# Window attention and a top-1 mixture of experts: a PSUM fill moved to TensorE, routing arithmetic moved to GpSimd

## The chip, the cores and the metric

One core of one Trainium2 chip. The metric is the device time of one execution in microseconds; of several executions the median is given.

## The reference, cut to what matters

Eight batches, eight heads, 576 positions, head size 64. Attention looks back over a window of 64 positions; its result, 4,608 rows of 512 numbers, goes through a gate that picks one of eight experts for each row, and only that expert's two matrices are applied.

```python
scores = scale * (q @ k.T)                      # per batch and head
scores = where((rel >= 0) & (rel < 64), scores, -1e9)
attn = softmax(scores); x = (attn @ v) as [4608, 512]
logits = x @ w_gate                             # [4608, 8]
e = argmax(logits, 1); g = softmax(logits)[e]
out[rows of e] = g * (relu(x[rows of e] @ w1[e]) @ w2[e])
```

## The kernel before, in words

**Attention.** The positions are cut into chunks of 64; two chunks make a tile of 128 rows, and there are 36 tiles. Step i of a loop written out by hand (L825 and on) works on several tiles at once, and the order of its calls is the order of each engine's queue. `scores(i)` on TensorE writes, for each chunk, its products with the chunk in front of it (half 0) and with itself (half 1) into PSUM. `folded(i)` on VectorE copies half 1 over half 0 where the mask says so (L412), `largest(i)` takes the maximum. ScalarE makes the exponentials of tile i-1 (L428) and copies the transposed ones of tile i-2 to SBUF (`tsb`, L437); GpSimd multiplies these by two masks (`pm`, L444, two instructions in each step); TensorE makes the products with v for tile i-3 (`values`, L458), and VectorE divides and writes `xrow` (`shares`, L468), which goes to DRAM. TensorE then transposes rows of tile i-4 (L475) and makes gate logits for every fourth step (L519).

The first chunk of each batch has no chunk in front of it. For these eight chunks `folded` first fills half 0 of their 64 partitions with FILL = -8e9 by a VectorE memset (L411). They fall in tiles 0, 4, 9, 13, 18, 22, 27 and 31.

**Routing.** After tiles 16, 28 and 36 (rounds of 16, 12 and 8 tiles; called round 1, 2 and 3 here) `route` turns logits into the row's place within its expert. It is cut into pieces `s1` to `s8`, which the loop takes from a queue `slow`, two in a step during attention and up to four after it: s1 the maximum `lm`; s2 the difference `ld` and the candidates `eq`; s3 the choice, as one-hot `oh`; s4 running counts on TensorE; s5 and s6 positions `pos` and the sum of exponentials; s7 and s8 the place and the gate weight in three bf16 parts (`val`). Then a queue `puts`, one entry in a step during attention and two after it, holds `put` (one-hot rows of the place within a block, `hot_row`, L601, four tiles each) and `early_parts` (`said`, L617); `follow` sets the steps in which a table of the first experts' rows is made (`early_table`) and in which GpSimd gathers these rows (`xg`, L179).

**Experts.** The first four experts' first two blocks of rows are begun inside the loop from step 36 (`forward`), the rest follows. Each weight tile is split into a rounded part `whi` (ScalarE) and a remainder `wlo` (VectorE, L237), and each product is made of three (L307, L311, L278). A planning stage (`plan`, VectorE, small instructions) places the remaining blocks.

`SPACE` is a tile that is never used; it keeps later tiles at the addresses they have.

Of the kernel before, what the change touches and what calls it, by code (L numbers as in the profile page):

```python
# [24 lines left out]
P = 128  # L25
# [39 lines left out]
RATE = (2, 1)  # L65
PUT = 4
AHEAD = 2
SPACE = (232, 64)
SPLIT = 26
TURN = 36  # L70
LAST = 7
# [47 lines left out]
def window_attention_then_top1_moe(ctx: ExitStack, tc: tile.TileContext, qkv, wall, wg, cst, out):  # L119
# [35 lines left out]
    def cc(name):  # L155
        o, w = CO[name]
        return cs[0][:, o:o + w] if o < NFIRST else cs[1][:, o - NFIRST:o - NFIRST + w]
# [8 lines left out]
    ones = const.tile([P, P], BF16, name="ones")  # L166
    one8 = const.tile([P, E], F32, name="one8")
    ones_f = const.tile([P, P], F32, name="ones_f")
    base = const.tile([P, E], F32, name="base")
    const.tile([P, SPACE[0]], F32, name="space0")  # L170
    xg = [const.tile([P, WIDE, C], F32, name=f"xg{i}") for i in range(3)]
# [25 lines left out]
    class Weights:  # L197
# [11 lines left out]
        def load(self):  # L209
            jj = self.loaded  # L210
            if jj == NJ // 2:
                return
            self.loaded += 1
            raw = self.raws[jj] = wr.tile([P, 2, 2 * C], F32, name="raw")
            ev = self.ev
            src = wall[ev, jj] if isinstance(ev, int) else wall[bass.ds(ev, 1), jj].rearrange("o p j f -> p (o j) f")
            if jj < self.spread:
                at, gap = QUARTERS[jj]
                quarters.extend((at + gap * k, raw[:, k // 2, k % 2 * C:(k % 2 + 1) * C],
                                 src[:, k // 2, k % 2 * C:(k % 2 + 1) * C]) for k in range(4))  # L220
            else:
                nc.sync.dma_start(out=raw, in_=src)
# [140 lines left out]
    nc.sync.dma_start(out=cs[1], in_=cst[:, NFIRST:])  # L363
    for c in range(6, FIRST):
        load(c)
    nc.vector.tensor_copy(out=fold, in_=cc("fold"))
    nc.vector.memset(ones, 1.0)
    nc.vector.memset(one8, 1.0)
    nc.vector.memset(ones_f, 1.0)
    for t in xg:  # L370
        nc.gpsimd.memset(t, 0.0)

# [19 lines left out]
    def scores(n):  # L392
        sp = sp_of(n)
        for g in range(NG):
            for j in range(2):
                c = 2 * n + j
                r = c % RING
                for a in range(2):
                    rows, cols = slice(a * W, (a + 1) * W), slice(j * W, (j + 1) * W)
                    if c % NC:  # L400
                        nc.tensor.matmul(sp[cols, a, g], lhsT=q_r[rows, r, g], rhs=k_r[rows, r - 1:r + 1, g], start=True,  # L401
                                         stop=True)
                    else:
                        nc.tensor.matmul(sp[cols, a, g, 1], lhsT=q_r[rows, r, g], rhs=k_r[rows, r, g], start=True, stop=True)

    def folded(n):

        sp = sp_of(n).rearrange("p a g b w -> p (a g) b w")
        for j in range(2):
            if (2 * n + j) % NC == 0:  # L410
                nc.vector.memset(sp[j * W:(j + 1) * W, :, 0], FILL)  # L411
        nc.vector.copy_predicated(out=sp[:, :, 0], mask=fold.unsqueeze(1).to_broadcast([P, H, W]), data=sp[:, :, 1])  # L412

    def largest(n):
# [108 lines left out]
    def route(nt, lgs, t0, rnd):  # L523
        def b8(x):
            return x.unsqueeze(2).to_broadcast([P, nt, E])

        v = {}

        def new(name, w=None, dt=F32):
            v[name] = rt.tile([P, nt] + ([w] if w else []), dt, name=name)  # L530
            return v[name]

        def s1():
            nc.vector.tensor_reduce(out=new("lm"), in_=lgs, op=ALU.max, axis=AX.X)

        def s2():
            nc.vector.tensor_tensor(out=new("ld", E), in0=lgs, in1=b8(v["lm"]), op=ALU.subtract)

            nc.vector.scalar_tensor_tensor(out=new("eq", E), in0=v["ld"], scalar=0.0,
                                           in1=cc("desc").unsqueeze(1).to_broadcast([P, nt, E]),  # L540
                                           op0=ALU.is_ge, op1=ALU.mult)
            new("ex", E)
            exs.append(lambda: nc.scalar.activation(out=v["ex"], in_=v["ld"], func=AF.Exp))

        def s3():
            nc.vector.tensor_reduce(out=new("em"), in_=v["eq"], op=ALU.max, axis=AX.X)
            oh = v["oh"] = rt.tile([P, nt + 1, E], BF16, name="oh")
            nc.vector.memset(oh[:, nt], 0.0)
            nc.vector.tensor_tensor(out=oh[:, 0:nt], in0=v["eq"], in1=b8(v["em"]), op=ALU.is_equal)

        def s4():
            oh = v["oh"]
            rk = rest_b[:, 1, 0:(nt + 1) * E].rearrange("p (t e) -> p t e", e=E)
            nc.tensor.matmul(rk, lhsT=tri, rhs=oh, start=True, stop=False)
            for s in range(1, nt + 1):
                nc.tensor.matmul(rk[:, s:], lhsT=ones, rhs=oh[:, 0:nt + 1 - s], start=False, stop=(s == nt))
            rks = v["rks"] = rt.tile([P, nt + 1, E], F32, name="rks")
            nc.scalar.copy(out=rks, in_=rk)

        def s5():  # L560
            rks = v["rks"]
            nc.vector.tensor_tensor(out=new("pos", E), in0=rks[:, 0:nt],
                                    in1=base.unsqueeze(1).to_broadcast([P, nt, E]), op=ALU.add)
            nc.vector.tensor_tensor(out=base, in0=base, in1=rks[:, nt], op=ALU.add)
            if rnd in SNAP:

                k = SNAP[rnd] // 2 * E
                nc.vector.tensor_tensor(out=base, in0=base, in1=cc("elow")[:, k:k + E], op=ALU.max)

        def s6():  # L570
            nc.vector.tensor_reduce(out=new("se"), in_=v["ex"], op=ALU.add, axis=AX.X)
            nc.vector.tensor_tensor(out=v["pos"], in0=v["pos"], in1=v["oh"][:, 0:nt], op=ALU.mult)
            nc.gpsimd.tensor_scalar(out=v["se"], in0=v["se"], scalar1=1e-9, scalar2=None, op0=ALU.add)

        ts_ = slice(t0, t0 + nt)

        def s7():
            nc.vector.tensor_reduce(out=new("pf2"), in_=v["pos"], op=ALU.add, axis=AX.X)
            nc.vector.reciprocal(out=new("g"), in_=v["se"])
            nc.gpsimd.tensor_scalar(out=new("fl"), in0=v["pf2"], scalar1=1.0 / P, scalar2=129.0 / 256,  # L580
                                    op0=ALU.mult, op1=ALU.add)
            nc.gpsimd.tensor_scalar(out=mid[:, ts_], in0=v["fl"], scalar1=RND, scalar2=RND + 1, op0=ALU.add,
                                    op1=ALU.subtract)

        def s8():
            nc.vector.scalar_tensor_tensor(out=new("lo"), in0=mid[:, ts_], scalar=float(-P), in1=v["pf2"],
                                           op0=ALU.mult, op1=ALU.add)

            nc.gpsimd.tensor_copy(out=val[:, ts_, 2], in_=v["g"])
            nc.gpsimd.tensor_tensor(out=new("g1"), in0=v["g"], in1=val[:, ts_, 2], op=ALU.subtract)  # L590
            nc.gpsimd.tensor_copy(out=val[:, ts_, 3], in_=v["g1"])
            nc.gpsimd.tensor_tensor(out=val[:, ts_, 4], in0=v["g1"], in1=val[:, ts_, 3], op=ALU.subtract)
            for t in range(0, nt, PUT):
                puts.append(lambda t=t: put(t, min(t + PUT, nt)))
            if rnd in SNAP:
                e0, rows = SNAP[rnd], t0 + nt
                puts.extend(early_parts(e0, rows))
                puts.append(lambda: follow(e0, rows))

        def put(a, b):  # L600
            nc.vector.tensor_tensor(out=hot_row[:, t0 + a:t0 + b], in0=rowb.unsqueeze(1).to_broadcast([P, b - a, P]),  # L601
                                    in1=v["lo"][:, a:b].unsqueeze(2).to_broadcast([P, b - a, P]), op=ALU.is_equal)


        again = (None,) if rnd + 1 < len(ROUNDS) else ()
        slow.extend((f in (None, s4), f) for f in (s1, s2, s3, *again, s4, s5, s6, s7, s8))
# [44 lines left out]
        fetch(xg[e % 3][:, u:u + 1], cols(eidx, [2 * e + u]), nt * P)  # L651

    def follow(e0, nt):
        i = rs_["step"] + 1 + (rs_["step"] >= NS)
        begin.append((i, lambda: early_table(e0, nt)))
        gets.extend((i + 1, lambda e=e, u=u: early_rows(e, u, nt)) for e in (e0, e0 + 1) for u in range(2))

# [170 lines left out]
    with tc.manual_schedule():  # L828
        keep_busy(BUSY[0])
        for i in range(NS + LAST):  # L830
# [60 lines left out]
            do("last")  # L891
            each(shares, i - 3)
            do("read")
            for k in range(RATE[0] if i < NS else 4):
                if slow and not slow[0][0]:
                    slow.popleft()[1]()
            for k in range(RATE[1] if i < NS else 2):
                if puts and not slow:
                    puts.popleft()()
            while lows:  # L900
                lows.popleft()()
            if pieces:
# [95 lines left out]
```

## Time and profile before

| | us |
|---|---|
| median of 3 runs (lowest to highest) | 645.65 (643.94 to 645.73) |
| the profiled execution | 645.74 |
| its span, first to last instruction | 644.0 |
| TensorE busy in it | 610.8 (95%) |
| VectorE busy | 396.5 (62%) |
| ScalarE busy | 361.3 (56%) |
| GpSimd busy | 195.6 (30%) |

Times in the trace are counted from the span's start; 1.7 us of the profiled execution lie outside its span. PE is TensorE's matmul, PEld its weight loads, DVE VectorE, ACT ScalarE, POOL GpSimd. TensorE's matmuls are pipelined, so its busy share says less than the places where it stands idle.

### The profile page before, as it was taken

The page shows a single profiled execution, that of the slowest core. Times are in us where ns is not written, and L with a number is a line of the kernel's source. Part 1 is how long each engine was busy: PE and PEld are TensorE (multiplying, and loading weights), DVE is VectorE, ACT ScalarE, POOL GpSimd, SP SyncE. Part 2 cuts the span into 40 slices and gives each one's busy share as a digit, 9 for nine tenths or more (in the row PEclk, how much of TensorE's full clock was granted, in tenths as well). Part 3 has the DMA queues.
Part 4 walks back from the last instruction along what each step waited for, and adds up shares of the span by engine and source line. Part 5 has one row for each costly group of instructions (what it writes and reads, how often), then busy time and mean ns, then how long its engine had stood idle before and what let it go on. Part 6 is the DMA issues. An engine that isn't in the chain of part 4 may idle for free.

```text
span 644.0 us, 16937 instructions
## 1 busy us (share of the span) xinstructions
PE 610.8 (95%) x6995; PEld 542.2 (84%) x6995; DVE 396.5 (62%) x707; ACT 361.3 (56%) x763; POOL 195.6 (30%) x180
## 2 busy tenths in 40 slices
PE   8798888898989999999999999999999999999995
PEld 4687777777868999889989999999999999999994
DVE  4666678996699565644446556565656555655651
ACT  4576666676354445635355565555565655556551
POOL 4666667578140431402112121221211311111011
PEclk9999999999999999999999999999999999999999
DMA  8988888954636578633447666665666666554621
GB/s 307 353 257 264 269 266 291 294 185 154 231 135 225 189 239 283 232 116 142 162 172 242 210 224 226 223 215 199 225 245 208 216 228 226 214 188 180 213 99 34
DMA packets 35110, 138.13 MB, mean 215 GB/s; under 512 B 4940, under 2 KB 6092, under 8 KB 25552
## 3 DMA queue, kind: packets, MB, share of 16 engines
q1 hardware_dynamic: 28624, 118.08, 53.6%
q0 software_dynamic: 6400, 18.88, 8.6%
q8 instruction: 57, 0.93, 0.6%
q14 instruction: 29, 0.24, 0.1%
HBM read 119.11 MB, written 19.92 MB: 216 GB/s over the span
## 4 chain that ended last, share of the span: by engine, by line
PE 74%; issue 10%; DVE 6%; POOL 6%; ACT 2%; POOLq 0%; ACTq 0%; DVEq 0%
PE e_b L307 20%; PE x_b L278 15%; PE e_b L278 14%; PE e_b L311 10%; POOL pm L444 5%; PE x_b L458 4%; PE s_b L401 3%; PE m_b L475 2%; PE m_b L519 1%; DVE wlo L237 1%; PE t_b L190 1%; PE m_b L190 1%; PE t_b L433 1%; DVE s_b L418 1%; DVE s_b L412 1%
## 5 line engine op out<-in xcount | busy, mean ns | idle before, releaser
L237 DVE TENSOR_TENSOR wlo<-raw,whi 128x1024 fp32r<-128x1024 f32 (+1 forms) x158 | 188.6, 1194 | 166.3 <-ACT whi L240 165.7
L240 ACT CAST whi<-raw 128x1024 fp32r<-128x1024 f32 (+1 forms) x153 | 155.2, 1015 | 106.9 <-PE x_b L278 55.8
L307 PE MATMUL e_b<-xh,whi 128*128 128x256 f32 (+1 forms) x480 | 127.3, 294 | 0.0
L307 PE MATMUL e_b<-xl,whi 128*128 128x256 f32 (+1 forms) x480 | 125.1, 290 | 0.2 <-DVE xl L193 0.2
L317 ACT ACTIVATE hh<-e_b 128x256 fp32r<-128x256 f32 (+1 forms) x152 | 60.3, 397 | 82.1 <-PE e_b L311 82.0
L444 POOL TENSOR_TENSOR pm<-tsb,cs 128x512 f32<-128x512 f32 x72 | 90.3, 1275 | 52.5 <-ACT tsb L437 41.3
L307 PEld LDWEIGHTS e_b<-xl,whi 128*128 128x128 f32 x480 | 90.9, 189 | 4.1 <-DVE xl L193 0.6
L307 PEld LDWEIGHTS e_b<-xh,whi 128*128 128x128 f32 x480 | 90.9, 189 | 3.6
L267 POOL DMA_INDIRECT out<-ys,idx_sb x32 | 38.6, 1207 | 177.5 <-ACT ys L266 172.9
L179 POOL DMA_INDIRECT xg<-xs,idx_sb x32 | 35.2, 1099 | 180.8 <-PE m_b L190 127.8
L311 PE MATMUL e_b<-xh,wlo 128*128 128x256 f32 (+1 forms) x480 | 79.8, 288 | 0.0
L318 DVE SCALAR_TENSOR_TENSOR hl<-e_b,hh 128x256 fp32r<-128x256 f32 (+1 forms) x152 | 65.7, 433 | 15.0 <-ACT hh L317 14.4
L428 ACT ACTIVATE pf<-s_b,mxs 128x64 f32<-128x64 f32 x288 | 62.9, 338 | 9.9 <-DVE mxs L420 8.3
L311 PEld LDWEIGHTS e_b<-xh,wlo 128*128 128x128 f32 x480 | 67.8, 188 | 0.0
L278 PE MATMUL x_b<-whi,hh 128*128 128x512 f32 x160 | 63.0, 394 | 0.8 <-ACT ys L266 0.8
L278 PE MATMUL e_b<-whi,hl 128*128 128x512 f32 x160 | 63.0, 394 | 0.6 <-DVE hl L318 0.6
L278 PE MATMUL x_b<-whi,hl 128*128 128x512 f32 x160 | 62.9, 393 | 0.4 <-DVE hl L318 0.4
L278 PE MATMUL x_b<-wlo,hh 128*128 128x512 f32 x160 | 62.9, 393 | 0.0
L278 PE MATMUL e_b<-wlo,hh 128*128 128x512 f32 x160 | 62.9, 393 | 0.0
L278 PE MATMUL e_b<-whi,hh 128*128 128x512 f32 x160 | 62.8, 393 | 0.0
L458 PE MATMUL x_b<-ring,pm 64*64 64x65 f32 x2176 | 46.6, 222 | 16.0 <-issue 7.0
L458 PEld LDWEIGHTS x_b<-ring,pm 64*64 64x64 f32 x2176 | 41.1, 134 | 21.9 <-issue 13.1
(160 smaller groups left out, 886.7 us busy)
## 6 DMA issues: line engine op xcount, KB each, us to landing
raw<-wall SPq DMA_DIRECT2D x74, 1024.0 KB, 5.1
ring<-qkv SPq DMA_DIRECT2D x66, 386.0 KB, 4.5
xs<-xrow SPq DMA_DIRECT2D x36, 256.0 KB, 3.1
raw<-wall SPq DMA_DIRECT2D x8, 256.0 KB, 5.0
ring<-qkv SPq DMA_DIRECT2D x4, 256.0 KB, 5.1
ring<-qkv SPq DMA_DIRECT2D x4, 130.0 KB, 5.1
ring<-qkv SPq DMA_DIRECT2D x1, 512.0 KB
xg<-xs,idx_sb POOLq DMA_INDIRECT x32, 3.9
```

The costliest lines, as they stand in the source:

```text
L179: nc.gpsimd.indirect_dma_start(out=t[:, u], out_offset=None, in_=xs[0:rows], in_offset=bass.IndirectOffsetOnAxis(ap=ix, axis=0), bounds_ch ...
L237: nc.vector.tensor_tensor(out=lo[:, s], in0=raw[:, s], in1=hi[:, s], op=ALU.subtract)
L240: nc.scalar.copy(out=hi[:, s], in_=raw[:, s])
L267: ins = nc.gpsimd.indirect_dma_start(out=out, out_offset=bass.IndirectOffsetOnAxis(ap=ix, axis=0), in_=ys, in_offset=None, bounds_check=N ...
L278: nc.tensor.matmul(y, lhsT=x[:, us], rhs=w[:, C:], start=(j == 0 and m == 0), stop=(j == NJ - 1 and m == 2))
L307: nc.tensor.matmul(hp[:, 0:w], lhsT=hi[:, ks], rhs=x[:, kk, 0:w], start=(kk == 0 and x is xh), stop=False)
L311: nc.tensor.matmul(hp[:, 0:w], lhsT=lo[:, kk * P:(kk + 1) * P], rhs=xh[:, kk, 0:w], start=False, stop=(kk == 3))
L317: nc.scalar.activation(out=hh[:, 0:w], in_=hp[:, 0:w], func=AF.Relu)
L318: nc.vector.scalar_tensor_tensor(out=hl[:, 0:w], in0=hp[:, 0:w], scalar=0.0, in1=hh[:, 0:w], op0=ALU.max, op1=ALU.subtract)
L428: nc.scalar.activation(out=pf[:, g, a], in_=sp[:, a, g, 0], func=AF.Exp, bias=mx[:, h:h + 1], scale=SCALE)
L444: nc.gpsimd.tensor_tensor(out=pm[i], in0=t.rearrange("p (g q) -> p g q", g=NG), op=ALU.mult, in1=cc("mask")[:, i * P:(i + 1) * P].unsqueez ...
L458: nc.tensor.matmul(x_b[cols, a, g * V1:(g + 1) * V1], lhsT=pm[i][rows, g, cols], rhs=v_r[rows, c % RING - i, g], start=(i == 0), stop=(i = ...
```

## The change

Four parts. The fill of half 0 for the eight chunks without a predecessor is no longer a memset: TensorE multiplies a tile `absent`, full of FILL / 64, by ones over 64 rows, right after the chunk's own product, eight calls for each such chunk. Seven instructions of `route` leave VectorE and come back as ten on GpSimd: `eq` and `lo` did two operations each and become two instructions, and the comparison that made `oh` becomes a difference and a comparison. Entries of `puts` are taken before pieces of `slow`, so that the first one-hot rows are made one step after s8, and `follow` is run together with the last entry in front of it. The unused tile shrinks by the 64 words that `absent` takes, and two memsets at the start change places.

```diff
-SPACE = (232, 64)
+SPACE = (168, 64)
...
+    absent = const.tile([P, W], F32, name="absent")
...
+    nc.vector.memset(ones, 1.0)
+    nc.vector.memset(ones_f, 1.0)
+    nc.vector.memset(absent, FILL / W)
     nc.vector.tensor_copy(out=fold, in_=cc("fold"))
-    nc.vector.memset(ones, 1.0)
     nc.vector.memset(one8, 1.0)
-    nc.vector.memset(ones_f, 1.0)
...
                         nc.tensor.matmul(sp[cols, a, g, 1], lhsT=q_r[rows, r, g], rhs=k_r[rows, r, g], start=True, stop=True)
+                        nc.tensor.matmul(sp[cols, a, g, 0], lhsT=absent[rows], rhs=ones_f[rows, 0:W], start=True, stop=True)
...
-        for j in range(2):
-            if (2 * n + j) % NC == 0:
-                nc.vector.memset(sp[j * W:(j + 1) * W, :, 0], FILL)
...
         def s2():
-            nc.vector.tensor_tensor(out=new("ld", E), in0=lgs, in1=b8(v["lm"]), op=ALU.subtract)
-
-            nc.vector.scalar_tensor_tensor(out=new("eq", E), in0=v["ld"], scalar=0.0,
-                                           in1=cc("desc").unsqueeze(1).to_broadcast([P, nt, E]),
-                                           op0=ALU.is_ge, op1=ALU.mult)
+            nc.gpsimd.tensor_tensor(out=new("ld", E), in0=lgs, in1=b8(v["lm"]), op=ALU.subtract)
+            nc.gpsimd.tensor_scalar(out=new("eq", E), in0=v["ld"], scalar1=0.0, scalar2=None, op0=ALU.is_ge)
+            nc.gpsimd.tensor_tensor(out=v["eq"], in0=v["eq"], in1=cc("desc").unsqueeze(1).to_broadcast([P, nt, E]),
+                                    op=ALU.mult)
...
             nc.vector.memset(oh[:, nt], 0.0)
-            nc.vector.tensor_tensor(out=oh[:, 0:nt], in0=v["eq"], in1=b8(v["em"]), op=ALU.is_equal)
+            nc.gpsimd.tensor_tensor(out=v["eq"], in0=v["eq"], in1=b8(v["em"]), op=ALU.subtract)
+            nc.gpsimd.tensor_scalar(out=oh[:, 0:nt], in0=v["eq"], scalar1=0.0, scalar2=None, op0=ALU.is_ge)
...
-            nc.vector.tensor_tensor(out=new("pos", E), in0=rks[:, 0:nt],
+            nc.gpsimd.tensor_tensor(out=new("pos", E), in0=rks[:, 0:nt],
                                     in1=base.unsqueeze(1).to_broadcast([P, nt, E]), op=ALU.add)
-            nc.vector.tensor_tensor(out=base, in0=base, in1=rks[:, nt], op=ALU.add)
+            nc.gpsimd.tensor_tensor(out=base, in0=base, in1=rks[:, nt], op=ALU.add)
...
-            nc.vector.tensor_tensor(out=v["pos"], in0=v["pos"], in1=v["oh"][:, 0:nt], op=ALU.mult)
+            nc.gpsimd.tensor_tensor(out=v["pos"], in0=v["pos"], in1=v["oh"][:, 0:nt], op=ALU.mult)
...
         def s8():
-            nc.vector.scalar_tensor_tensor(out=new("lo"), in0=mid[:, ts_], scalar=float(-P), in1=v["pf2"],
-                                           op0=ALU.mult, op1=ALU.add)
+            nc.gpsimd.tensor_scalar(out=new("lo"), in0=mid[:, ts_], scalar1=float(-P), scalar2=None, op0=ALU.mult)
+            nc.gpsimd.tensor_tensor(out=v["lo"], in0=v["lo"], in1=v["pf2"], op=ALU.add)
...
-                puts.append(lambda: follow(e0, rows))
+                puts.append(lambda f=puts.pop(): (f(), follow(e0, rows)))
...
-        i = rs_["step"] + 1 + (rs_["step"] >= NS)
+        i = rs_["step"] + 1
...
+            for k in range(RATE[1] if i < NS else 2):
+                if puts and not slow:
+                    puts.popleft()()
             for k in range(RATE[0] if i < NS else 4):
                 if slow and not slow[0][0]:
                     slow.popleft()[1]()
-            for k in range(RATE[1] if i < NS else 2):
-                if puts and not slow:
-                    puts.popleft()()
```

## Rows read from the trace of the kernel before

**Rows 1.** Busy time by stretch: us, PE, PEld, DVE, ACT, POOL, clock, DMA, GB/s.

```profile
80.00:120.00 40.00, 35.19 (x1102) 30.21 (x1095) 32.64 (x84) 27.43 (x102) 25.79 (x27) 1.00 0.87 280
320.00:640.00 320.00, 316.52 (x2045) 287.67 (x2044) 180.96 (x238) 180.36 (x267) 56.07 (x49) 1.00 0.58 200
```

**Rows 2.** The chain of waits, 60 to 160 us: start, length, what.

```profile
143.94 2.51 POOL pm L444 x2
146.49 1.09 PE x_b L458 x55
```

**Rows 3.** TensorE's timeline where it stood idle, idle time and releaser in brackets.

```profile
44.79 1.41 PE L458 MATMUL x_b<-ring,pm 64*64 64x65 f32 x64 [0.49 <-DVE xrow L468]
...
77.31 1.15 PE L458 MATMUL x_b<-ring,pm 64*64 64x65 f32 x59 [0.41 <-issue]
...
96.85 1.16 PE L458 MATMUL x_b<-ring,pm 64*64 64x65 f32 x64 [0.50 <-DVE xrow L468]
```

**Rows 4.** Timeline: scores of a tile without a fill, and of tile 13 with one.

```profile
21.01 1.10 PE L401 MATMUL s_b<-ring 64*64 64x128 f32 x32
...
22.25 0.70 DVE L412 COPY_PREDICATED s_b<-fold,s_b 128x512 f32<-128x512 int32 x1 [0.53 <-PE s_b L401]
...
57.20 0.38 PE L401 MATMUL s_b<-ring 64*64 64x128 f32 x4
...
57.88 0.48 DVE L411 MEMSET s_b<- 64x512 f32 x1 [0.57 <-PE s_b L404]
...
58.40 0.69 DVE L412 COPY_PREDICATED s_b<-fold,s_b 128x512 f32<-128x512 int32 x1
```

**Rows 5.** Groups of instructions by shape, 0 to 160 us: busy us, mean ns, idle before.

```profile
L444 POOL TENSOR_TENSOR pm<-tsb,cs 128x512 f32<-128x512 f32 x72 | 90.3, 1275 | 52.5 <-ACT tsb L437 41.3 <-PE x_b L458 5.8 <-PE s_b L401 4.8
...
L617 DVE TENSOR_TENSOR said<-here,val 128x320 bf16<-128x320 bf16 x1 | 0.5, 539 | 0.0
...
L592 POOL TENSOR_TENSOR val<-g,val 128x16 bf16<-128x16 f32 x1 | 0.2, 239 | 0.1
...
L580 POOL TENSOR_SCALAR fl<-pf 128x16 f32<-128x16 f32 x1 | 0.2, 210 | 0.6 <-DVE pf L578 0.6
```

**Rows 6.** Timeline, round 2, the steps of s1 to s3.

```profile
138.09 0.25 DVE L534 TENSOR_REDUCE lm<-lgs 128x12 f32<-128x96 f32 x1
...
138.23 1.23 POOL L179 DMA_INDIRECT xg<-xs,eidx  x1 [0.16 <-DVE lgs L504]
...
140.04 2.49 POOL L444 TENSOR_TENSOR pm<-tsb,cs 128x512 f32<-128x512 f32 x2 [0.58 <-PE m_b L475]
...
142.69 1.21 POOL L179 DMA_INDIRECT xg<-xs,eidx  x1 [0.16 <-issue]
```

**Rows 7.** Timeline, round 1, the steps of s1 to s3.

```profile
89.05 0.29 DVE L534 TENSOR_REDUCE lm<-lgs 128x16 f32<-128x128 f32 x1
...
90.69 2.50 POOL L444 TENSOR_TENSOR pm<-tsb,cs 128x512 f32<-128x512 f32 x2 [1.97 <-PE x_b L458]
...
94.10 1.27 POOL L444 TENSOR_TENSOR pm<-tsb,cs 128x512 f32<-128x512 f32 x1 [0.90 <-ACT tsb L437]
```

**Rows 8.** Timeline, round 3: the maximum and the first count.

```profile
171.77 0.22 DVE L534 TENSOR_REDUCE lm<-lgs 128x8 f32<-128x64 f32 x1
...
173.46 0.21 PE L554 MATMUL x_b<-oh,tri 128*128 128x72 bf16 x1
```

**Rows 9.** Timeline after s8 of round 3.

```profile
180.06 1.21 DVE L237 TENSOR_TENSOR wlo<-raw,whi 128x1024 fp32r<-128x1024 f32 x1
180.29 1.06 POOL L592 TENSOR_TENSOR val<-g,val 128x8 bf16<-128x8 f32 x1
...
181.33 0.75 PE L311 MATMUL e_b<-xeh,wlo 128*128 128x256 f32 x4 [1.35 <-DVE wlo L237]
```

**Rows 10.** TensorE's busy time in short stretches: us, PE, clock, DMA, GB/s.

```profile
28.00:30.00 2.00, 0.58 (x34) 1.00 0.87 306
30.00:32.00 2.00, 2.00 (x20) 0.52 0.55 124
```

## The prediction

> **What bounds the kernel now.** I read the busy shares by stretch first, then the chain of waits, then the places where TensorE stood idle. The stretches show two regimes. In the expert stage TensorE is busy 316.5 of 320 us; nothing of the change runs there, so it keeps its length and only starts sooner or later. In the attention stage no engine is full: VectorE 32.6 of 40 us, GpSimd 25.8, TensorE 35.2 [rows 1]. There a step is a loop through all four engines, and what arrives last differs from step to step. The chain of waits shows one place that matters for this change: in round 2 it runs through GpSimd's two masks and from there into TensorE's products with v [rows 2]. The idle places of TensorE tell the rest: in the steps after tiles 9, 13 and 22, all three with a fill, it waited some 0.5 us for VectorE's `xrow` (first and last of the three); after tile 18, with a fill too, it waited for nothing that the profile shows [rows 3]. So VectorE and GpSimd are late in turn, and work moved from the one to the other pays only where the first is last and the second has room.
>
> **The sum is made against the profiled execution,** 645.74, that is 0.09 over the median of 645.65. About 0.3% (1.9 us) is what a measurement of this kernel can tell from no change.
>
> **The fill.** In a plain tile `folded` starts 0.14 us after the scores end (21.01 + 1.10 to 22.25). In tile 13 the scores end at 57.58, the memset starts at 57.88, and the copy at 58.40, so 0.82 after; the fill costs 0.68 us on VectorE's path [rows 4]. In its place TensorE does eight calls of 64 columns, two passes each as with the other scores (32 instructions for 16 calls), so 16 passes. The trace has no such product by constants; the nearest row is 32 passes of scores in 1.10 us, so 16 passes are 0.55 us or, if they slip between passes that other parts of the array hold up, nothing [rows 4]. I take the row's 0.55, as the new pass stands right behind one in the same part of the array. Then `folded` starts 0.13 sooner, and TensorE's stream is 0.55 longer. Tiles 9, 13 and 22, where VectorE was last: -0.13 each, -0.4. Tile 18: of 0.55, the wait of 0.41 that follows swallows what it can, +0.1. Tile 27: I take +0.1 on the same grounds. Tiles 0, 4 and 31: nothing, since TensorE waits for data or masks behind them; without that cover 0.55 each. Together -0.2. Bounds: -1.5 if the products are free and the three waits of 0.5 go [rows 3], +3.9 if seven fills each cost TensorE 0.55. The two swapped memsets at the start and the smaller unused tile cost nothing: TensorE's first products need only `ones`, which is first in either order, and addresses stay.
>
> **Prices on GpSimd.** A product of 512 elements takes 1275 ns, one of 16 takes 239: 2.09 ns for an element and 206 ns for the start [rows 5]. So two-input instructions take 0.47 us (round 1, 128 elements), 0.41 (round 2, 96) and 0.34 (round 3, 64). For a comparison with a constant on so many elements there is no row; it lies between the 0.21 of 16 elements and the two-input price, and I take the middle: 0.34, 0.31, 0.28. Between neighbours lie 0.04 us (142.69 + 1.21 to 143.94) [rows 2, 6].
>
> **Round 1.** s2 puts three instructions on GpSimd behind `lm` and ahead of the next masks: 0.47 + 0.34 + 0.47 and three gaps, 1.40. `lm` ends at 89.34, so they end near 90.8; the masks began at 90.69, so +0.1. s3 puts 0.47 + 0.34 + 0.08 = 0.89 between 93.19, the end of those masks, and 94.10, the start of the next: it fits, but the 0.1 stays [rows 7]. In s5 and s6 three instructions follow the masks, and VectorE's maximum over `base` now waits for GpSimd's sum; behind it in VectorE's queue stand the sum of exponentials and the next copy of logits. I take another +0.1 for this and for the two instructions of `lo`, which stand ahead of masks in s8, while VectorE no longer waits there and makes `hot_row` a step later. Together +0.2; bounds -0.5 (VectorE freed of the wait in row 96.85) and +1.0.
>
> **Round 2.** Here GpSimd also issues a gather in each step, and it is on the chain. The gather ends at 139.46, the masks start at 140.04: 0.58 of room. `lm` ends at 138.34, before the gather, so s2 goes into that room whole: 0.41 + 0.31 + 0.41 and three gaps, 1.25, less 0.58: +0.67. In the next step masks, gather and masks stand back to back (140.04 + 2.49, 142.69 + 1.21, then 143.94) [rows 2, 6], so s3's 0.41 + 0.31 + 0.08 = 0.80 is added whole. TensorE's products wait for the second of these masks (143.94 + 2.51, then 146.49) and so start 1.5 us later. Nothing behind them gives this back: from there TensorE's chain goes on. The second gather starts 0.7 later; it feeds transposes two steps on, which start later by more. Bounds: +0.8, if all five cost 0.24 (1.4 with gaps, less 0.58); +1.5 is near the other end, as the prices are, but for the rival below.
>
> **Round 3.** After step 36 there are no more scores. s1 to s3 run in one step: `lm` ends at 171.99; 0.34 + 0.28 + 0.34 on GpSimd, then the maximum on VectorE (0.22, as `lm`), then 0.34 + 0.28, with gaps and three handovers of about 0.08 (my estimate) `oh` is there near 174.2. TensorE's first count started at 173.46 and stands in its queue ahead of expert products, so it stalls 0.7 us [rows 8]. Behind these five instructions stand the gathers of step 41; their rows are for the third expert, and the second stands before it, which hides 3 us; without that cover the delay of some 2 us would be TensorE's. The gain: s7 and s8 are followed by two `hot_row` and then by `wlo`; TensorE waited 1.35 for that `wlo` [rows 9]. With VectorE's wait for `lo` and the `hot_row` a step later, `wlo` starts sooner, but VectorE waits for GpSimd's products in s6, and in the last step the two `hot_row` are paid in front of the next `wlo`. I take half, -0.6. Together +0.1; bounds -1.35 and +0.7.
>
> **The later one-hot rows.** They begin in steps 25, 37 and 42 where they began in 24, 36 and 41. Because `follow` no longer takes a step of its own, the tables stay in steps 31 and 40, and the gathers in theirs. The last part, `said`, now ends one step ahead of its table; its 0.54 [rows 5] would stand in front of the table's products if it came late, and TensorE's expert products or scores cover it. Taken at nothing.
>
> **Sum:** -0.2 + 0.2 + 1.5 + 0.1 = +1.6, so 645.74 + 1.6 = 647.3 us, 0.26% over the median. The forecast is a small loss within what can be told from no change.
>
> **Rival 1: faster, VectorE is the one that arrives last.** If the products of constants are free for TensorE, the three waits of 0.5 go (-1.5), and if `wlo` in round 3 comes in time, 1.35 go [rows 3, 9]; GpSimd then costs 0.8 in round 2. That is -2.0, so 643.7. For it speaks that all three waits stand behind fills. Against it: the added passes stand in TensorE's queue right in front of what waits. It decides where 16 passes cost under 0.2 us.
>
> **Rival 2: clearly slower, GpSimd is held up by VectorE.** A GpSimd instruction of 8 elements took 1.06 us while VectorE's `wlo` ran beside it, ending 0.08 after it, where one of 16 elements took 0.24 in the clear [rows 5, 9]. So an instruction may stand until VectorE's is through, 0.8 us more. In round 3 `wlo` stands right behind the maximum in VectorE's queue; if it comes between the two instructions of `oh`, TensorE's stall is 0.7 + 1.2 (one `wlo`), and round 3 is +1.3 instead of +0.1. One such hold in each of s2 and s3 of round 2, behind quarter pieces of `wlo` of some 0.4, adds 0.8. With the sum that is +3.6: 649.3. Against it: most routing runs while VectorE works on PSUM, and the masks kept their 1275 ns there. It decides from the first held instruction on the chain. The Trainium skill (GPSIMD Engine Reference, Key points) says that GpSimd shares its SBUF interfaces with VectorE and contends with VectorE instructions that have two SBUF inputs or run in a two-port mode; `wlo` reads `raw` and `whi`, and by that rule every new pair meets this. The 1.06 agrees.
>
> **Rival 3: no change, by the clock.** From 30 to 32 us TensorE was granted 0.52, the lower level of 1.2 GHz, after it had been busy for 0.58 of 2 us [rows 10]. At the lower level these 2 us did 1.04 of work. If a few tenths of added passes in tile 4 shift the idle time ahead of it, the other 0.96 comes back: 646.3, nearer to no change than the forecast. Nothing in the change aims at it.
>
> **How the numbers follow.** Forecast 0.43, rival 1 0.22, rival 2 0.24, rival 3 0.11. The forecast's own range, 646.2 to 648.4, lies four fifths under the bound of 647.6 and one fifth over it, since two of its prices are taken in the middle; so 0.09 of its 0.43 is slower. Slower: 0.24 + 0.09 = 0.33, and I put 0.03 of rival 3 there, where a second low stretch appears: 0.36. Same: 0.34 + 0.08 = 0.42. Faster: 0.22. The range takes in rival 1 with a little of the free bounds (-2.5) and rival 2 with some of the fills' upper bound (+4.3): 643.2 to 650.0.
>
> **What would show it.** Right: `pm` near 143.94 starts some 1.5 us later relative to the gather before it, with five short GpSimd instructions in the gaps; TensorE's waits for `xrow` after tiles 9, 13 and 22 shrink by little; the first count of round 3 waits for GpSimd; the wait of 1.35 for `wlo` is gone or halved. Wrong: scores with absent chunks no longer than the others; masks in round 2 not later; GpSimd's comparisons near 0.2 or over 0.5 us; a low-clock stretch gone or doubled.

## The result, and the profile after

The changed kernel took 652.72 us (median of 4, 650.93 to 654.26) where the kernel before took 645.26 beside it: ratio 1.0118 [1.0086, 1.0149]. Two more measurements, a_again and a_third below, gave 1.0109 and 1.0109. The mean of the three, 1.0112, is +7.2 us; 647.3 was forecast, with a range that ended at 650.0. The profiled execution took 654.26, its span is 651.8 and its mean granted clock (the share of full clock that TensorE was given) 0.987, where the span before was 644.0 at 0.995. Line numbers of the changed kernel are higher by a few: `keep_busy` is L385, scores are L403, L406 and, new, L407, `xg` L180, `wlo` L238.

The busy shares by stretch, as in [rows 1]:

```profile
80.00:120.00 40.00, 36.13 (x1082) 31.57 (x1085) 29.31 (x73) 27.18 (x102) 30.00 (x37) 0.96 0.86 276
320.00:640.00 320.00, 320.00 (x2065) 291.38 (x2064) 184.06 (x241) 181.18 (x268) 54.09 (x47) 1.00 0.58 202
```

The move itself shows: VectorE fell by 3.3 us in 40 and GpSimd rose by 4.2. What the kernel lost it lost before the expert stage: `lm` of round 3 starts at 176.79 instead of 171.77 [rows 8], and TensorE's products of L753, in front of that stage, start at 201.61 instead of 193.83, 7.8 us later. From there to the end both kernels take 450.2 us.

What TensorE waited for says where to look. First the table of waits of the kernel before, 0 to 150 us (engine, line, releaser: us in total, times, longest):

```profile
PE x_b L458 <- POOL pm L444: 3.3, 8, 0.8
PE x_b L458 <- DVE xrow L468: 2.8, 5, 1.0
```

The same of the changed kernel; it has no row for `xrow` at all:

```profile
PE x_b L458 <- POOL pm L444: 6.3, 12, 1.3
```

In this stretch the waits for `xrow` went, all 2.8 us of them. Those for GpSimd's masks grew by 3.0, and all rows of the two tables add to some 18 us in both kernels. TensorE is 3.3 us behind near the end of this stretch (the first count of round 2, L554, starts at 147.58 and at 150.88 in the two chains of waits). So in these two executions longer work, and not more waiting, put it behind there; what was added are the products of the fill and, as told below, more time at the lower clock.

**Round 1.** GpSimd's, VectorE's and TensorE's timelines in the steps of s7 and s8 (the row at 109.91 is one of the four masks by itself):

```profile
107.08 0.27 POOL L586 TENSOR_SCALAR lo<-mid 128x16 f32<-128x16 f32 x1
107.43 0.22 POOL L587 TENSOR_TENSOR lo<-lo,pf 128x16 f32<-128x16 f32 x1
...
108.68 5.40 POOL L444 TENSOR_TENSOR pm<-tsb,cs 128x512 f32<-128x512 f32 x4
...
109.13 1.37 DVE L601 TENSOR_TENSOR hot_row<-rowb,lo 128x512 bf16<-128x512 bf16 x1
...
109.91 1.72 POOL L444 TENSOR_TENSOR pm<-tsb,cs 128x512 f32<-128x512 f32 x1
...
111.68 1.07 PE L458 MATMUL x_b<-ring,pm 64*64 64x65 f32 x56 [1.33 <-POOL pm L444]
```

Eight short instructions stand ahead of the masks, two of them new, and four masks then run without a pause. TensorE waits 1.33 for the second of the four, which took 1.72 us, from 109.91 to 111.63, where a mask takes 1.28 in the mean; `hot_row` ran on VectorE until 110.50 of that. In the kernel before, TensorE waited in the same step too, for `xrow`:

```profile
109.35 1.50 PE L458 MATMUL x_b<-ring,pm 64*64 64x65 f32 x64 [1.03 <-DVE xrow L468]
```

**Round 2.** The chain of waits, as in [rows 2], and in it the steps of [rows 6]:

```profile
141.81 2.50 POOL pm L444 x2
...
144.46 1.11 POOL xg L180
...
145.60 0.36 POOL eq L548
...
146.05 0.45 POOL oh L549
...
146.50 2.47 POOL pm L444 x2
...
149.02 1.03 PE x_b L458 x45
```

Masks, gather, `eq`, `oh` and masks stand back to back on the chain, as forecast. The gather of the step before, from GpSimd's timeline:

```profile
139.17 1.26 POOL L180 DMA_INDIRECT xg<-xs,eidx  x1 [0.17 <-issue]
```

It ends at 140.43, and the masks that TensorE waits for start at 146.50, 6.07 later. In the kernel before these two lie at 139.46 and 143.94, 4.48 apart [rows 2, 6]. So the masks start 1.6 later relative to that gather.

The prices, from the groups by shape (busy us, mean ns):

```profile
L538 POOL TENSOR_SCALAR eq<-ld 128x128 f32<-128x128 f32 x1 | 0.6, 553 | 0.1
...
L538 POOL TENSOR_SCALAR eq<-ld 128x96 f32<-128x96 f32 x1 | 0.5, 466 | 0.1
...
L537 POOL TENSOR_TENSOR ld<-lgs,lm 128x128 f32<-128x128 f32 x1 | 0.4, 408 | 0.7 <-DVE lm L534 0.7
...
L538 POOL TENSOR_SCALAR eq<-ld 128x64 f32<-128x64 f32 x1 | 0.4, 376 | 0.1
...
L537 POOL TENSOR_TENSOR ld<-lgs,lm 128x96 f32<-128x96 f32 x1 | 0.4, 368 | 0.0
...
L537 POOL TENSOR_TENSOR ld<-lgs,lm 128x64 f32<-128x64 f32 x1 | 0.3, 298 | 12.7 <-DVE lm L534 12.7
```

**Round 3.** The timeline from the maximum to the first count, as in [rows 8]:

```profile
176.79 0.22 DVE L534 TENSOR_REDUCE lm<-lgs 128x8 f32<-128x64 f32 x1
...
177.09 0.30 POOL L537 TENSOR_TENSOR ld<-lgs,lm 128x64 f32<-128x64 f32 x1 [12.68 <-DVE lm L534]
...
178.28 0.22 DVE L545 TENSOR_REDUCE em<-eq 128x8 f32<-128x64 f32 x1 [1.28 <-POOL eq L539]
178.43 1.22 DVE L238 TENSOR_TENSOR wlo<-raw,whi 128x1024 fp32r<-128x1024 f32 x1
...
178.58 1.22 POOL L548 TENSOR_TENSOR eq<-eq,em 128x64 f32<-128x64 f32 x1 [0.33 <-DVE oh L547]
...
179.89 0.37 POOL L549 TENSOR_SCALAR oh<-eq 128x64 bf16<-128x64 f32 x1
...
180.31 0.19 PE L554 MATMUL x_b<-oh,tri 128*128 128x72 bf16 x1 [1.67 <-POOL oh L549]
```

The difference L548 took 1.22 us; `wlo` ran from 178.43 to 179.65 beside it, and L548 ended 0.15 after. The first count waits 1.67. The wait of 1.35 for `wlo` in [rows 9] is gone: TensorE's waits for `wlo` from 165 to 200 us were 1.6 us before and are 0.2 now.

**The clock.** TensorE's busy time, its granted clock, DMA share and GB/s in 2 us each, as in [rows 10]:

```profile
24.00:26.00 2.00, 2.00 (x67) 0.50 1.04 412
26.00:28.00 2.00, 2.00 (x40) 0.69 0.57 165
...
112.00:114.00 2.00, 2.00 (x58) 0.64 0.84 305
114.00:116.00 2.00, 2.00 (x42) 0.50 0.70 205
...
156.00:158.00 2.00, 1.89 (x67) 0.74 0.39 143
158.00:160.00 2.00, 2.00 (x11) 0.50 0.05 22
...
180.00:182.00 2.00, 1.69 (x13) 0.71 0.55 152
182.00:184.00 2.00, 2.00 (x8) 0.50 0.98 410
```

Half clock is the lower level of 1.2 GHz. The four stretches follow waits: one of 2.45 for nothing that the profile shows, ending at 23.58, the 1.33 for a mask, one of 1.93 for `xrow` ending at 156.11, and the 1.67 ending at 180.31. A wait alone does not bring the level, though: the kernel before waited 1.74 for `xrow` in the same place (ending at 152.62) and kept full clock behind it. Before there was one such stretch, at 30 to 34 (0.52, [rows 10], and then):

```profile
32.00:34.00 2.00, 2.00 (x56) 0.62 0.95 289
```

By these rows (the share of clock that is missing, times 2 us) the four stretches cost 6.4 us of work and the one before 1.7. So 4.7 of the 7.8 us between these two executions can be clock. That is more than in most: the changed kernel's 16 runs had a mean granted clock of 0.991, and this one 0.987.

### The profile page after: what moved, and what is told of

It reads as the page before. It is cut to its first block, busy times and chain, and to the rows that moved or that the text cites. A ratio compares the mean times of both kernels' runs of the same rounds, so it can differ in the third digit from the quotient of the medians.

```text
span 651.8 us, 17188 instructions
## 1 busy us (share of the span) xinstructions
PE 617.1 (95%) x7123; PEld 547.9 (84%) x7123; DVE 389.2 (60%) x679; ACT 361.0 (55%) x763; POOL 205.5 (32%) x210
## 4 chain that ended last, share of the span: by engine, by line
PE 74%; issue 10%; POOL 7%; DVE 5%; ACT 3%; POOLq 0%; ACTq 0%; DVEq 0%
PE e_b L308 20%; PE x_b L279 15%; PE e_b L279 14%; PE e_b L312 10%; POOL pm L444 5%; PE x_b L458 4%; PE s_b L403 3%; PE m_b L475 2%; PE m_b L519 1%; PE t_b L191 1%; PE m_b L191 1%; ACT pf L428 1%; DVE wlo L238 1%; PE t_b L433 1%; ACT xT L482 1%
## 5 line engine op out<-in xcount | busy, mean ns | idle before, releaser
L238 DVE TENSOR_TENSOR wlo<-raw,whi 128x1024 fp32r<-128x1024 f32 (+1 forms) x158 | 188.3, 1192 | 163.8 <-ACT whi L241 152.3
L180 POOL DMA_INDIRECT xg<-xs,idx_sb x32 | 35.1, 1098 | 180.8 <-PE m_b L191 127.7
```

The source lines that it names most:

```text
L180: nc.gpsimd.indirect_dma_start(out=t[:, u], out_offset=None, in_=xs[0:rows], in_offset=bass.IndirectOffsetOnAxis(ap=ix, axis=0), bounds_ch ...
L238: nc.vector.tensor_tensor(out=lo[:, s], in0=raw[:, s], in1=hi[:, s], op=ALU.subtract)
```

## The experiments

Four theories have letters in the expectations. A: the routing on GpSimd is late in round 2 and held by `wlo` in round 3, with the low clock that follows. B: the fill on TensorE. C: the later one-hot rows. D: any routing on GpSimd costs, wherever it stands. Ratios are to the kernel before, run in turn with each on the same chip; its medians there were 645.6 to 646.9. Single runs of one kernel spread over 3 to 10 us (before: 642.6 to 652.3 in all), so I read ratios with their intervals.

### The parts alone

The fill alone (e1_fill, and the same again as e9_fill_again and e15_fill_third) is the kernel before with the tile `absent` and

```diff
+                        nc.tensor.matmul(sp[cols, a, g, 0], lhsT=absent[rows], rhs=ones_f[rows, 0:W], start=True, stop=True)
...
-                nc.vector.memset(sp[j * W:(j + 1) * W, :, 0], FILL)
```

> The kernel before with the fill on TensorE alone; routing and one-hot rows as before. Theory A (the loss is GpSimd's routing in rounds 2 and 3, late in its queue or held by VectorE, and the low clock that TensorE's waits bring after it): within 2 us of the kernel before, 644 to 647. Theory B (the loss is the fill: longer scores in eight steps, and 256 more instructions in TensorE's stream that bring low-clock stretches): 649 to 653.

> The kernel before with the fill on TensorE alone, once more, to narrow its interval beside the four-fold one. If the fill is covered: ratio 0.998 to 1.004 again. If the difference between the changed kernel and the one without its fill (0.6% in two calls) is the fill's: 1.004 to 1.008.

> Fill on TensorE alone for the third time (1.0011 and 1.0031 so far). Prediction's step: -0.2 us (ratio 0.9997). Theory B (TensorE's 128 products of constants stand on the path): +1 to +2 us (ratio 1.002). If taking it out of the whole is what it costs in itself (+4 us, ratio 1.006), the earlier two were low.

Measured: 1.0011 [0.998, 1.0043], 1.0031 [1.0011, 1.0052], 1.0053 [1.0028, 1.0077]; 12 runs each. The mean is 1.0032, +2.0 us. One measurement would have misled in either direction: the first lies with theory A, the third nearest to the 1.006 that was given for the fill's share in the whole.

The routing with the later rows, filled by memset (e2_route, again as e13_route_again), has these two lines the other way round. The later rows alone (e3_rows) have VectorE's routing and the memset:

```diff
-                nc.gpsimd.tensor_tensor(out=new("ld", E), ...)
+                nc.vector.tensor_tensor(out=new("ld", E), ...)
```

and so on through s8. e14_fill_rows is e3_rows with the fill on TensorE.

> The changed kernel with the fill by memset again; routing on GpSimd and later one-hot rows stay. Theory A: 650 to 653, nearly all of the loss stays. Theory B: 644 to 647.

> The changed kernel with the fill by VectorE's memsets, measured a second time, on the chip of the unchanged change. If the parts add: +3 us (ratio 1.0046), and the difference to the whole is the fill's +1.5 us. If fill and routing cost more together than apart: still +3 us, with the whole at +7 us, so that taking the fill away gives back 4 us.

> The kernel before with the later one-hot rows alone. Theories A and B: within 2 us of the kernel before, and if anything faster, since two hot_row leave the place ahead of the wlo for which TensorE waited 1.35 us. Theory C (the later rows push VectorE's planning back): 647 or more.

> Fill on TensorE and the later one-hot rows, all routing on VectorE as before. If the later rows are free also beside the fill (prediction): the fill's cost alone, +0.7 to +2 us (ratio 1.001 to 1.003). If rows and fill together carry what the parts measured apart do not show: about +3 us (ratio 1.005), as with fill, rows and round 1's routing together (1.0053).

Measured: e2_route 1.0046 [1.0022, 1.007], e13_route_again 1.0045 [1.0017, 1.0073], so +2.9 us; e3_rows 0.9997 [0.9973, 1.0021]; e14_fill_rows 1.0029 [1.0007, 1.005], no more than the fill alone. The median of e2_route, 649.4, lies between the ranges of A and B, each of which had the whole loss in one part. Theory C falls; A or D, and B, each stand for a part.

The whole change again, a_again and a_third:

> The changed kernel itself once more, beside the others of this call, since single runs spread over some 6 us. All theories: 651 to 654. It is the measure for the three below.

> The changed kernel once more, so that the next two stand beside it. If its parts simply add (fill about +1.5 us, routing about +3.0 us, later rows 0), it is at about +4.5 us (ratio 1.007); if something that only the whole kernel has costs 2 to 3 us more (theory: more low-clock stretches when fill and routing are together), it is at +7 us again (ratio 1.011).

Measured: 1.0109 [1.0082, 1.0136] and 1.0109 [1.0067, 1.0152]. Fill and routing measured apart add to +4.9 us, the whole is at +7.2.

### What a product of constants costs

e8_fill4 is the fill alone with every such product made four times, into the same place:

```diff
+                        for _ in range(4):
+                            nc.tensor.matmul(sp[cols, a, g, 0], lhsT=absent[rows], rhs=ones_f[rows, 0:W], start=True, stop=True)
```

> The kernel before with the fill on TensorE alone, each of its products made four times over (the same values are written again). The time per set of eight fills is a third of what this adds to the fill made once. If a set stands on TensorE's path at 0.4 to 0.55 us for a tile in the seven tiles behind the start: 3 sets add 8 to 12 us, 654 to 658. If TensorE's waits cover most of it: 647 to 650.

Measured: 1.0209 [1.0174, 1.0244]. Against the fill's 1.0032 three more sets cost 0.0177, 11.4 us: 3.8 us a set, 0.48 in each of the eight tiles, 30 ns for each of the 16 passes that a tile takes. The median, 660.5, lies over both ranges given; the 11.4 lies in the 8 to 12 of the first.

### Which round

e4_r12 takes round 3's routing back to VectorE, e5_r1 rounds 2 and 3, e10_r2 only s2 and s3 of round 2; e16_fill_r1 is e5_r1 with the one-hot rows as before. The form, for e4_r12:

```diff
+            if rnd in (0, 1):
                 nc.gpsimd.tensor_tensor(out=new("ld", E), in0=lgs, in1=b8(v["lm"]), op=ALU.subtract)
...
+            else:
+                nc.vector.tensor_tensor(out=new("ld", E), in0=lgs, in1=b8(v["lm"]), op=ALU.subtract)
```

> The changed kernel with the routing of round 3 on VectorE again, rounds 1 and 2 on GpSimd. Theory A: the wait of 1.67 us ahead of round 3's first count goes, and with it the low-clock stretch behind it (about 1.6 us): 3 us under the changed kernel, 648 to 650. If round 3 costs only its wait: 1.7 us under it. Theory B: no different from the changed kernel, 651 to 654.

> The changed kernel with the routing of rounds 2 and 3 on VectorE; round 1, the fill and the later rows stay as changed. Theory A (rounds 2 and 3 make the loss): 645 to 647. Theory D (any routing on GpSimd together with the fill makes it, since the steps of round 1 lose as well): 649 to 652.

> The changed kernel with s2 and s3 of round 2 alone on VectorE, five GpSimd instructions fewer in front of its masks. Theory A: the masks of tile 32 follow the gather at once again, TensorE starts 1.5 to 2 us sooner, and 650 to 651.5 results. If round 2's instructions are covered: as the changed kernel, 652 to 653.

> Fill on TensorE and round 1's routing on GpSimd, one-hot rows in their old place. If round 1 is free (prediction +0.2): as the fill alone, +1 to +2 us (ratio 1.002). If round 1 beside the fill is what the extra 1.5 us of the three together (1.0053) is: about +3 us (ratio 1.005).

Measured: e4_r12 1.0099 [1.0061, 1.0137], too wide to tell; e5_r1 1.0053 [1.003, 1.0075], so rounds 2 and 3 carry 0.0059 of the whole's mean of 1.0112, 3.8 us; e10_r2 1.0084 [1.0054, 1.0113], 0.0025 less than a_again, 1.6 us, of which the intervals leave the sign open; e16_fill_r1 1.0072 [1.0037, 1.0107].

Not all of this fits. The median of e5_r1, 650.0, lies in the range of theory D and over that of theory A, which had left no room for the fill's 2.0 us. The median of e10_r2, 652.3, lies in the range for instructions that are covered. And e16_fill_r1 is over both its ratios. Round 1 beside the fill costs 0.0040 by e16_fill_r1 (less the fill's mean) and 0.0024 by e5_r1 (less e14_fill_rows), 2.6 and 1.6 us; neither difference is clear of noise. That stays open.

### The held comparison

e6_behind is the changed kernel with the two `wlo` of steps 40 and 41 put behind round 3's counts; nothing else moves:

```diff
-            while lows:
+            while lows and i != NS + LAST - 3:
                 lows.popleft()()
...
                 f = slow.popleft()[1]
                 if f:
                     f()
+                while lows:
+                    lows.popleft()()
```

e11_r2_behind is this and e10_r2 together. e12_route_mended is e11_r2_behind with the fill by memset.

> The changed kernel with the two wlo of step 40 and 41 put behind round 3's counts in VectorE's queue, so that none runs beside GpSimd's differences, comparisons and places. If wlo holds GpSimd's instruction: the difference of 64 elements takes 0.3 us instead of 1.22, the first count waits 0.7 us instead of 1.67, the conversion to mid takes 0.26 instead of 1.10; 1 to 3 us less in all. If 1.22 has another cause: durations and time as in the changed kernel.

> Both: s2 and s3 of round 2 on VectorE, and the two wlo behind round 3's counts. Theory A: the two gains add, 3 to 4 us under the changed kernel, 648 to 650. If both only move a wait to another place: 651 or more.

> The changed kernel with the fill by VectorE's memsets as before, the differences, comparisons and products of round 2 back on VectorE, and the two least-significant-part subtractions of steps 40 and 41 put behind round 3's counts. Theory A (the routing's cost is round 2's chain and round 3's held comparison, about 1.9 us each): nothing of the routing's cost is left, 0 to +0.5 us to the kernel before (ratio 1.000 to 1.001). Theory D (any routing on GpSimd costs, wherever it stands): about +3 us as with the memset fill alone (ratio 1.0046).

The timeline of e6_behind at the same place:

```profile
177.38 0.29 POOL L548 TENSOR_TENSOR eq<-eq,em 128x64 f32<-128x64 f32 x1 [0.33 <-DVE oh L547]
...
177.76 0.37 POOL L549 TENSOR_SCALAR oh<-eq 128x64 bf16<-128x64 f32 x1
...
178.18 0.19 PE L554 MATMUL x_b<-oh,tri 128*128 128x72 bf16 x1 [0.74 <-POOL oh L549]
178.29 2.35 DVE L238 TENSOR_TENSOR wlo<-raw,whi 128x1024 fp32r<-128x1024 f32 x2
```

The same instruction takes 0.29 with nothing beside it, and the wait falls from 1.67 to 0.74. The conversion to `mid` (L582), held in the same way further on, takes 0.25 instead of 1.10. Measured: e6_behind 1.008 [1.0051, 1.011], 0.0029 or 1.9 us less than a_again, with intervals that overlap; e11_r2_behind 1.0052 [1.0029, 1.0074], 0.0057 or 3.7 us less, clear of noise, so the two gains add (its median, 650.6, lies between the two ranges given); e12_route_mended 1.0008 [0.9984, 1.0032], against 1.0045 for e13_route_again on the same chip. These two intervals overlap; with e2_route's 1.0046 beside them the difference of 0.0037 is more than the 0.003 that the intervals together allow. With round 2's s2 and s3 back and `wlo` out of the way, the rest of the routing on GpSimd costs nothing that can be told beside memsets. So theory D falls in the form that e12_route_mended tested. In the form of e5_r1, routing beside the fill, it stays open. Theory A stands for the two places together, without its clause on the clock.

### The clock behind a wait

e7_busy puts eight idle products ahead of round 3's first count, so that TensorE does not stand still there:

```diff
                 f = slow.popleft()[1]
+                if i > NS:
+                    keep_busy(8)
                 if f:
```

> The changed kernel with eight products of ones by ones on TensorE ahead of round 3's first count, which fill the wait there and are read by nobody. If the low clock behind the count follows from the wait: no stretch at the lower level within 5 us behind the count, and the profile gains 1.6 us there; the median 0 to 2 us less. If the clock falls for other reasons: a stretch at the lower level stays, and the time is that of the changed kernel or up to 0.5 more.

Measured: 1.0083 [1.0053, 1.0112]. No low stretch follows the count. But a_again has none there either, with a wait of 1.66 in the same place, ending at 177.30. Ten us from the count, in the changed kernel's first profile and in a_again:

```profile
180.00:190.00 10.00, 9.69 (x59) 0.83 0.43 157
```

```profile
177.00:187.00 10.00, 9.61 (x69) 1.00 0.45 157
```

So e7_busy tells nothing about the clock: the same wait brings the low level in one execution and not in the next.

## Why the prediction was wrong, by its own steps

**The fill: -0.2 forecast, +2.0 measured.** The price was right: 0.55 for a tile's products against 0.48 measured. VectorE's waits for `xrow` shrank, as rival 1 had it: in the first 150 us they were 2.8 before, and 0.8, 0.8 and 1.0 in three profiles with the fill alone. The step that failed is what was set against the price. I let five tiles pay 0.1 or nothing ("Tiles 0, 4 and 31: nothing") and three gain 0.13, on the ground that TensorE waits for others there; that takes some 4.6 us of cover and gain in all (eight times 0.55, and 0.2). With 3.8 for a set of products and 2.0 for the whole fill, 1.8 came, or 0.23 for each tile. What e8_fill4 prices are sets two to four, which may no longer find the cover that the first one had; so whether the 1.8 is the memsets' or cover, and which tiles pay, no run shows. The measured cost lies inside the bounds given, -1.5 to +3.9, nearer the upper.

**Round 1: +0.2 forecast, open.** s2 and s3 fit into the gaps as forecast: TensorE waited 0.24 and 0.23 for masks in their steps, in the second of them in place of the 0.50 for `xrow` in [rows 3]. In the step of s7 and s8 it had waited 1.03 for `xrow`, a wait that the prediction did not count, and now waited 1.33 for a mask. Counted from `fl` (L580), which starts at 105.12 before and at 106.43 after, the first mask starts 0.10 later, so the "+0.1" for `lo` held. The second mask ends 0.57 later, since it took 1.72 beside `hot_row`. This is the hold of rival 2, with another VectorE instruction of two SBUF inputs, in a step where the prediction had it in no term. A mask of 1.71 or 1.72 stands in the same place in a_again, a_third and e12_route_mended. What round 1 costs on balance is nothing that can be told beside memsets (e12_route_mended, which has it) and 1.6 to 2.6 us, not clear of noise, beside TensorE's fill. Of the 2.6 in e16_fill_r1 some 2.0 can be the clock: its mean granted clock was 0.9904, the lowest of all, against 0.9935 with the fill alone. That the two press on the same steps, one holding TensorE's stream back and one its masks, is an argument and not shown.

**Round 2: +1.5 forecast, and by the trace 1.6.** The masks start that much later relative to the gather, as forecast. The times agree, 1.6 (a_again less e10_r2) and, with `wlo` moved, 1.8 (e6_behind less e11_r2_behind); but the interval of each takes in nothing, so that they come out so close is luck. Two-input instructions were cheaper than forecast (0.37 for 0.41), comparisons dearer (0.47 for 0.31); over the five instructions that is 0.18 more, too little to tell in a measurement. None of the five was held.

**Round 3: +0.1 forecast; the hold alone is 1.9, with intervals that overlap.** The stall forecast without a hold was 0.7, and 0.74 is what e6_behind shows once `wlo` is out of the way. What failed is that the hold stood outside the sum. It was rival 2, at the place and with the instruction named there: `wlo` follows the maximum in VectorE's queue, and the difference behind `oh` stands until it is through. I gave it 0.24 although the row that showed it, 1.06 us of an 8-element instruction beside a `wlo` [rows 9], was on the page. Of the 1.9, 0.93 is the shorter wait of the first count; where the rest lies is not shown. By the Trainium skill (GPSIMD Engine Reference, Key points) GpSimd contends with VectorE instructions that have two SBUF inputs; 1.22 against 0.29 here and the mask of 1.72 bear that out. The masks' mean of 1275 ns, which I held against it, hid such cases. The other half of the step was wrong as well. The wait for `wlo` did go, but e3_rows, with no routing on GpSimd, loses most of it too (1.6 to 0.5 us of such waits from 165 to 200 us), so it came from the later rows, and a wait of 0.7 for `xrow` came in its stead. With e3_rows at 0.9997, nothing was gained.

**Later rows: nothing forecast, nothing measured** (0.9997; and 1.0029 against the fill's 1.0032).

**The clock: rival 3 had the wrong sign.** The low stretch at 30 us went, but another came at 24, and there are three more; I had put 0.03 on a second one. The mean granted clock over all runs was 0.9946 before (119 runs), 0.9935 with the fill, 0.9936 with the routing and 0.9914 with both (16). From before to both that is 0.0032 of 650 us, 2.1 us if all of it is lost time; fill and routing lose 0.7 each when alone. So some 0.7 of the 2.3 by which the whole exceeds its parts can be the clock. The rest, 1.6, is no more than the half-widths of the ratios allow (0.002 to 0.004 each, or 1.3 to 2.6 us). Which wait brings which low stretch stays open.

**The sum, as measured:** fill 2.0, routing 2.9, of which the two places in rounds 2 and 3 make all that can be told, rows 0, and 2.3 that only the whole kernel shows; 7.2. So the steps that failed are the cover for the fill and the hold that stood outside the sum; and the parts, which the prediction added, do not quite add, by little more than the intervals allow, and the cause of that stays open. No version here is shown to beat the kernel before.

## What to carry to other kernels

An engine that waits now and then does not cover work put into its stream at other places. Here products priced at 3.8 to 4.4 us were forecast to cost nothing on balance and left 2.0: begin with the full price of added products, and take off only a wait that ends last behind each of them.

Before moving short instructions to GpSimd, look at what VectorE runs at that moment: one long instruction with two SBUF inputs turned 0.3 us into 1.2, and moving that instruction behind the handover brought TensorE's wait from 1.67 to 0.74. Look for single long cases and not at a mean: a mean of 1275 ns held a mask of 1.53 in the kernel before, and one of 1.72 after.

Two profiles of kernels that differ by one per cent can differ more by clock than by the change: 4.7 of 7.8 us here.

## What the hardware showed that I had not expected

On GpSimd a comparison with one constant costs more than a difference of two tiles of the same shape: 0.55, 0.47 and 0.38 us for 128, 96 and 64 elements, against 0.41, 0.37 and 0.30. I had placed it below.

The hold goes both ways: beside these masks `hot_row` took 1.37, and 0.69 in the kernel before at 105.94, where no mask ran.

The same kernel is granted one low-clock stretch in one execution (a_again) and four in another, 0.995 and 0.987 of full clock on average, and this change moved the mean over many runs by 0.003.
